# Splitting the output projection of the last attention units, and giving late scores more PSUM tiles

## The chip, the cores and the metric

The kernel runs on one core of a Trainium2 chip. The metric is the device time of one execution in microseconds (us); lower is better. The core's engines work side by side: TensorE (PE, matrix products, with PEld for its weight loads), VectorE (DVE), ScalarE (ACT), GpSimd (POOL) and SyncE (SP, which issues every DMA of this kernel).

## The reference

Two independent results of 2048 x 448 are placed side by side. The first is a state space layer, the second an attention layer with 16 heads of 28:

```python
# a: a kernel K (448 x 2048) made from the parameters, then a long convolution
P = jnp.exp((A * dt[:, None])[:, :, None] * pos[None, None, :])
K = 2.0 * jnp.einsum("dn,dnl->dl", C, P).real
y = jnp.fft.irfft(jnp.fft.rfft(u_t, 4096) * jnp.fft.rfft(K, 4096)[None], 4096)[:, :, :2048]
a = y.transpose(0, 2, 1) + u * D_skip
# b: softmax attention, then the output projection
q, k, v = (x @ wqkv)...                       # 16 heads of 28
p = softmax(q @ k.T * 28 ** -0.5)
b = (p @ v).reshape(B, S, 448) @ wo
out = concatenate([a, b], axis=-1)
```

## The kernel before

The attention is cut into 16 **units**: four groups `g` of four heads times four chunks `c` of 512 queries, `u = 4 g + c`. A unit is walked in 16 **steps** of 128 keys, so that there are 256 steps `s` in one long loop. In a step, for each of the four heads, `s_mm` makes a 128x512 score tile `pss` in PSUM on PE and ACT takes its exponential into `p`. `pv_step` multiplies the `p` of the step before with the values into `po`. Some units ahead of the scores, `max_mm` makes the same scores once more for the row maxima, which DVE (and for some ACT) reduce into `mx`. In the last 18 steps there are no maxima left to make: there the flag `late` is set.

Between these products stand **slots**. The order of one step is written out in `ORDER = ('m0', 's0', 'm1', 's1', 'v', 'f', 'pv', 'f', 'v', 'k', 'm2', 's2', 'm3', 's3', 'v')`: `s` is a score, `m` a maximum, `f` a slot. So one slot stands ahead of `pv_step` and one behind it. In `late` steps a third slot stands at the end of the step. Each slot takes one piece of work, in this order of preference (function `slot`):

1. the `urgent` pieces: the end of a unit's maxima, and `sums` and `scale`, which divide a finished unit's result by its softmax sums and give the tile `on`;
2. `p_due`: the pieces of the output projection that are due at this step;
3. other due lists, empty by the last four units;
4. `f_slot("s")`: the next piece of a **spectrum** job of the convolution;
5. `f_slot("f")`: the next piece of a **finish** job of the convolution.

There are 16 spectrum jobs of four pieces each: two `forth` (products with `yk`, which DVE multiplies into `pr`; behind the second one `join` makes `p` on DVE and POOL), one slot later than the next the two `back` (products of `p`, copied by ACT into `y` and stored to `z`). There are 8 finish jobs of four calls `one(i)` each: a product of `zi` on PE, and an addition of `ut` on DVE into `ot`, which is stored in two halves. Ahead of a job's first call POOL multiplies `ut` with the skip weights. The finish jobs of a half can only start when the eight spectrum jobs of that half are done.

The inputs of a job are loaded by `f_load`, which is called when the job before it has started, and at the earliest three steps (finish) or two steps (spectrum) before the job's own start. The loads of a finish job are `zi` (896 KB) and `ut` (two DMAs, 448 KB together). All DMAs stand in SP's one queue in the order of the program. After the last step the remaining pieces are worked off slot by slot.

Each unit of the last group (`u` = 12 to 15) ends with the output projection of its 512 queries. `load_og(u)` loads the results of the three other groups (`og`, 768 KB); `project(t)` makes, for 128 queries, the products of all four groups with `wo` into one PSUM tile, ACT copies it to `y`, and SP stores it. Each `mm32` product is four matmuls in the program, eight in the trace. So one `project` is 24 matmuls on `og` and 8 on `on` in the trace.

PSUM has eight tiles of 128x512. In this part of the kernel the scores take three in turn (`ps_s`), `po` has one, and four (`w_tile`) serve the maxima and everything in slots. All instructions of this part are kept in the order of the program. They all carry line L75 in the profile, the line of a recording helper, so rows are told apart by tiles.

Of the kernel before, what the change touches and what calls it, by code (L numbers as in the profile page):

```python
# [8 lines left out]
F32 = mybir.dt.float32  # L9
F32R = mybir.dt.float32r  # L10
I32 = mybir.dt.int32
AF = mybir.ActivationFunctionType
ALU = mybir.AluOpType
# [5 lines left out]
D = 448  # L19
# [3 lines left out]
G = 4  # L23
HG = H // G
CQ = 512
NQ = L // CQ
# [10 lines left out]
FX, PD, GAP = 1, 2, 2  # L37
FL = {"s": 2, "f": 3}
S0, SP, SW, SD, PW, E3 = 0, 4, 0, 5, 37, 8
UG = (2, 2, 4)  # L40
PS = 1
SGB, XB, XL = 2, 5, 4
K0, KP, KD, UP = 0, 3.5, 4, 3
A0, A1, KW = 26, 34, (33, 35, 36)
# [46 lines left out]
def body(ctx, tc, a, out):  # L91
    nc = Engines(tc)
    nc.kept = KEPT["p"]
    x, wqkv, wo, u_a = a["B_x"][0], a["B_wqkv"], a["B_wo"], a["A_u"][0]
    out = out[0]

    def pool(stack, name, bufs=1, space=None, side=None):
        kw = {} if space is None else {"space": space}
        if side:
            kw["side"] = side  # L100
        return stack.enter_context(tc.tile_pool(name=name, bufs=bufs, reuse_waits="tile", **kw))
# [23 lines left out]
    def w_tile():  # L125

        n_ring[0] += 1
        return ps_w[0].tile([128, CQ], F32, name=f"pm{n_ring[0] % ps_w[1]}")
# [7 lines left out]
    def mm32(o, w, x_, start, stop, at=0):  # L136

        for i in range(w.shape[-1] // 32):
            c = slice(32 * i, 32 * i + 32)
            nc.tensor.matmul(o[c], w[:, c], x_, start=start, stop=stop, tile_position=(0, at + 32 * i))  # L140
# [13 lines left out]
    def load_v(g, c):  # L154
        v_g[g, c] = t = v_p.tile([128, NK // NQ, HG, 32], F32, name="v", bufs=5)
        nc.sync.dma_start(t.rearrange("p t h e -> p t (h e)"), v_d[c][:, g])
# [55 lines left out]
    with ExitStack() as st:  # L212
# [47 lines left out]
        t = a["A_log_dt"]  # L260
# [261 lines left out]
        def project():  # L522

            e = work.pop(0)() if work else None
            while pend:
                pend.pop(0)()
            if e:
                pend.append(e)
# [29 lines left out]
    ps_s = pool(att, "ps_s", 3, PSUM)  # L558
# [6 lines left out]
    late = [False]  # L565
# [136 lines left out]
    wo_t = []  # L702
# [9 lines left out]
            wo_t.append(t)  # L712

    def s_mm(u, kt, j):
        pss = ps_s.tile([128, CQ], F32, name="pss")
        nc.tensor.matmul(pss, kt_g[u // NQ][j][:, kt * 128:(kt + 1) * 128], q_u[u][:, j, :], start=True, stop=True)
        p = kq_p.tile([128, CQ], F32, name="p", bufs=PB)
        nc.scalar.activation(p, pss, AF.Exp, scale=SCALE)
        return p
# [8 lines left out]
    og_u = {}  # L728

    def load_og(u):  # L730
        og_u[u] = og = kq_p.tile([128, G - 1, CQ], F32, name="og")
        nc.sync.dma_start(og, on_d[u % NQ][:G - 1].rearrange("g p q -> p g q"))

    def fin(u, s_):
        g, c = divmod(u, NQ)
        o = kq_p.tile([128, CQ], F32, name="o")
        nc.scalar.activation(o, o_u[u], AF.Copy)
        on = kq_p.tile([128, CQ], F32, name="on", bufs=2)
        rb = kq_p.tile([128, 4, HG, 32], F32, name="rb")
        og = og_u.pop(u, None)  # L740

        def sums():
            pw = w_tile()
            for t in range(4):
                mm32(pw[:, t * HG:(t + 1) * HG], o[:, t * 128:(t + 1) * 128], sel, start=True, stop=True)
            r = kq_p.tile([128, 4, HG], F32, name="r", bufs=2)
            nc.vector.reciprocal(r, pw[:, :4 * HG].rearrange("p (t h) -> p t h", h=HG))
            nc.scalar.activation(rb, r[:, :, :, None].to_broadcast([128, 4, HG, 32]), AF.Copy)

        def scale():  # L750
            pw = w_tile()
            for t in range(4):
                mm32(pw[:, t * 128:(t + 1) * 128], rb[:, t].rearrange("p h e -> p (h e)"), ident, True, True)
            nc.vector.tensor_tensor(on, o, pw, ALU.mult)
            if g < G - 1:
                nc.sync.dma_start(on_d[c][g], on)
            else:
                p_due.extend((s_ + PD + PS * t, lambda t=t: project(t)) for t in range(4))

        def project(t):  # L760
            pw = w_tile()
            ts = slice(t * 128, (t + 1) * 128)
            for g2 in range(G):
                mm32(pw[:, :D], og[:, g2, ts] if g2 < G - 1 else on[:, ts], wo_t[g2 // 2][:, g2 % 2, :],
                     start=g2 == 0, stop=g2 == G - 1)
            y = kq_p.tile([128, D], F32, name="y", bufs=2)
            nc.scalar.activation(y, pw[:, :D], AF.Copy)
            q0 = c * CQ + t * 128
            nc.sync.dma_start(out[q0:q0 + 128, D:], y)

        soon_slot(UG[1], sums)
        soon_slot(UG[2], scale)

    fk = {}
# [102 lines left out]
    def u_part(i, c):  # L877
        u_jobs[i][1 + c]()
        if c and i not in (14, 15):
            u_load(i + 2)  # L880
        if c and i == 15:
            u_load(16)
            u_load(17)
        if c and i == 31:
            load_wo()
# [15 lines left out]
    f_p, f_ready = {}, {}  # L901

    p_due = collections.deque()
# [37 lines left out]
    def soon_slot(gap, f):  # L941
        n_urgent[0] += 1
        urgent.append((n_slot[0] + gap, n_urgent[0], f))
        q = sorted(urgent)
        urgent.clear()
        urgent.extend(q)

    def slot(s_):
        n_slot[0] += 1
        if urgent and urgent[0][0] <= n_slot[0]:  # L950
            urgent.popleft()[2]()
        elif s_ >= NS and f_slot(s_, "s"):
            pass
        elif p_due and p_due[0][0] <= s_:
            p_due.popleft()[1]()
        elif m_due and m_due[0][0] <= s_:
            m_due.popleft()[1]()
        elif u_due and u_due[0][0] <= s_:
            u_part(*u_due.popleft()[1:])
        else:  # L960
            f_slot(s_, "s") or f_slot(s_, "f")
# [35 lines left out]
    for s in range(NS):  # L997
        u, kt = divmod(s, NK)
        sm = s + NK + min(LEAD, 1 + s // 2)
        more = s in (2, 4)  # L1000
        if s == 12 * NK:
            k0_st.close()
            f_p["s", 0] = f_p["s", 1] = pool(f0_st, "f0_p", side="right")
            f_ready["s", 0], f_ready["s", 1] = s, NS
        if s >= 12 * NK and f_ready["s", 1] == NS and not (k_due or m_due or powers["g"] or powers["e"]):
            g_st.close()
            ps_st.close()
            ps_w[:] = pool(ps_st, "ps_f", 4, PSUM), 1
            f_ready["s", 1] = s + F1
        if kt == 12 and u // NQ == G - 1:  # L1010
            load_og(u)
        late[0] = s + NK + LEAD > NS
        if u % NQ == NQ - 1 and u < NU - 1 and kt % 4 == 2:
            load_v(u // NQ + 1, kt // 4)
        if sm < NS and sm // NK % NQ == NQ - 1 and sm % NK % 4 == 0 and sm % NK and sm // (NQ * NK) + 1 < G:
            load_kd(sm // (NQ * NK) + 1, sm % NK // 4 - 1)
        if sm < NS and sm % (NQ * NK) == 0 and sm:
            load_kd(sm // (NQ * NK), HG - 1)
        if kt % 4 == 1 and u % NQ == 1 and u // NQ + 1 < G:
            load_k(u // NQ + 1, kt // 4, k_pools[(u // NQ + 1) % 2])  # L1020
        if kt == 2:
            if u + 2 < NU:
                load_q(u + 2)
        ps = []
        for op in ORDER:
            if op[0] == "s":
                ps.append(s_mm(u, kt, int(op[1])))
            elif op[0] == "f":
                slot(s)
            elif op[0] == "v":  # L1030
                vec()
            elif op == "k":
                k_next()
                k_begin(s)
                for _ in range(1 if s else 2):
                    k_seed(s)
                for _ in range(3):
                    if powers["e"]:
                        powers["e"].popleft()()
            elif op == "pv":  # L1040
                if prev:
                    pv_step(*prev)
                    if prev[1] == NK - 1:
                        fin(prev[0], s)
            elif sm < NS:
                max_mm(sm // NK, sm % NK - more, int(op[1]))
        for kc in range(4 if more else 0):
            max_mm(1, sm % NK, kc)
        for _ in range(FX if late[0] else 0):
            slot(s)  # L1050
        if sm < NS and sm % NK == NK - 1:
            def end(un=sm // NK):
                max_end(un, w_tile())
                max_put(un)
            max_join(sm // NK)
            soon_slot(UG[0], end)
        k_next()
        prev = (u, kt, ps)
    pv_step(*prev)
    fin(prev[0], NS)  # L1060
    s = NS
# [63 lines left out]
```

## Time and profile before

| | |
|---|---|
| time, median of 3 runs | 1335.06 us (1334.6 to 1336.06) |
| span of the profiled execution | 1335.5 us |
| PE busy | 1238.7 us (93%) |
| DVE, ACT, POOL busy | 990.8, 954.3, 839.3 us |
| mean granted PE clock | 0.972 |
| DMA engines, share of the span | 55.0% for the queue of the kernel's own DMAs |

The profiled execution's span, from its first to its last instruction, lies 0.4 us above the median. In a row of the timeline the first number is the start in us from the span's start, the second the time from the start of the first to the end of the last of the instructions merged into the row, then engine, line, operation, tile written and tiles read, shapes and count; a bracket gives the idle time before it and what ended it. Matmuls overlap, so the distance between two starts tells more of the cost of a piece than the second number. In a row of the windows, each engine's busy time stands in the order PE, PEld, DVE, ACT, POOL, then the granted PE clock, the share of the DMA engines and the GB/s.

### The profile page before, as it was taken

Reading aid. Unit: us, or ns where it says so; the run is one execution under the profiler, and the core shown is the slowest. Engines: PE = TensorE matmul, PEld = TensorE weight load, DVE = VectorE, ACT = ScalarE, POOL = GpSimd, SP = SyncE. Lnnn points to the kernel's source line nnn. Section 1 sums busy time; section 2 is a strip of 40 time slices with the busy share of each in tenths; the row PEclk is TensorE's granted clock in tenths of the full one; section 3 lists DMA queues with packets and bytes.
Section 4 is the critical chain, followed back from the end, with each engine's and each line's share of the span. In section 5 each row is a group of like instructions: output and inputs, shape, how many; then the busy total and the mean of one; then the engine's idle time right before and its main releaser. Section 6 shows DMA issues by size and latency. Waiting matters only on the chain.

```text
span 1335.5 us, 33195 instructions
## 1 busy us (share of the span) xinstructions
PE 1238.7 (93%) x12625; PEld 705.5 (53%) x12625; DVE 990.8 (74%) x2138; ACT 954.3 (71%) x2068; POOL 839.3 (63%) x704
## 2 busy tenths in 40 slices
PE   6879985899999999999989999999998999898998
PEld 5657763455555555555545555555555545444433
DVE  5897887877787777777768889889886858657311
ACT  4875862477788888888878888888885656555553
POOL 3675681388688888788789989999992202202211
PEclk9889987899999999999999999999998999999999
DMA  6677769726765546468634234642424554825485
GB/s 192 208 263 250 240 205 286 202 63 138 177 153 131 113 137 179 129 171 223 165 79 106 61 71 92 143 99 66 100 56 140 191 156 136 256 102 166 149 215 142
DMA packets 200088, 205.36 MB, mean 154 GB/s; under 512 B 95992, under 2 KB 158520, under 8 KB 197880
## 3 DMA queue, kind: packets, MB, share of 16 engines
q1 hardware_dynamic: 199928, 203.23, 55.0%
q8 instruction: 100, 1.64, 0.5%
q14 instruction: 60, 0.49, 0.1%
HBM read 120.73 MB, written 82.18 MB: 152 GB/s over the span
## 4 chain that ended last, share of the span: by engine, by line
PE 67%; DVE 14%; DMA 6%; ACT 5%; POOL 4%; issue 3%; SPq 1%; ACTq 0%; POOLq 0%; DVEq 0%
PE pm L75 37%; PE pss L75 15%; PE po L75 15%; DVE mx L75 2%; DVE tri L75 2%; DMA sdb<-sd 2%; DVE p L75 2%; DVE pr L75 1%; POOL qhat L75 1%; ACT p L75 1%; SPq L75 1%; DVE rl L75 1%; ACT tri L75 1%; DVE qhat L75 1%; DVE sg L75 1%
## 5 line engine op out<-in xcount | busy, mean ns | idle before, releaser
L75 ACT ACTIVATE p<-pss 128x512 f32<-128x512 f32 x1024 | 561.6, 611 | 122.2 <-PE pss L75 117.4
L75 PE MATMUL pss<-qhat,khat 128*128 128x512 f32 x1024 | 405.0, 402 | 10.8 <-ACT p L75 10.6
L75 DVE TENSOR_REDUCE mx<-pm 128x1 f32<-128x512 f32 x500 | 321.5, 684 | 102.8 <-PE pm L75 101.3
L75 PE MATMUL pm<-khat,qhat 128*128 128x512 f32 x749 | 327.5, 439 | 14.7 <-DVE mx L75 7.3
L75 POOL TENSOR_TENSOR e<-e,sdb 128x256 f32<-128x256 f32 x168 | 201.7, 1201 | 134.1 <-ACT e L75 121.3
L75 PE MATMUL po<-p,v 128*32 128x512 f32 x2048 | 271.0, 598 | 0.0
L75 POOL TENSOR_TENSOR e<-e,eu 128x256 f32<-128x256 f32 x168 | 248.3, 1478 | 13.2
L75 PEld LDWEIGHTS pm<-khat,qhat 128*128 128x128 f32 x749 | 141.7, 189 | 212.7 <-ACT p L75 44.4
L75 DVE CUSTOM_DVE_ANT_0 rl<-pm,rl 128x512 f32<-128x512 f32 x249 | 171.5, 689 | 70.7 <-ACT rl L75 64.9
L75 PEld LDWEIGHTS pss<-qhat,khat 128*128 128x128 f32 x1024 | 191.4, 189 | 59.1 <-ACT p L75 19.9
L75 POOL TENSOR_TENSOR eu<-e,sdb 128x256 f32<-128x256 f32 x168 | 202.0, 1202 | 0.0
L75 ACT ACTIVATE rl<-pm 128x512 f32<-128x512 f32 x249 | 151.2, 607 | 20.9 <-PE pm L75 16.5
L75 POOL TENSOR_TENSOR p<-pr,pr 64x448 f32<-64x448 f32 x32 | 40.9, 1278 | 199.0 <-DVE pr L75 187.9
L75 DVE TENSOR_TENSOR g<-g,zg 128x128 f32<-128x128 f32 x392 | 162.1, 414 | 3.5
L75 PE MATMUL pm<-xh,khat 112*128 112x512 f32 x256 | 94.1, 451 | 22.8 <-DVE hl L75 11.0
L75 PE MATMUL pm<-kdif,qhat 128*128 128x512 f32 x249 | 101.0, 405 | 3.4 <-DVE mx L75 1.8
L75 DVE TENSOR_TENSOR zg<-g,zg 128x128 f32<-128x128 f32 x224 | 87.9, 392 | 5.0
L75 PEld LDWEIGHTS pm<-e,g 128*32 128x32 f32 x3584 | 57.5, 110 | 42.1 <-issue 19.4
L75 PEld LDWEIGHTS pm<-xh,khat 112*128 112x128 f32 x256 | 54.1, 217 | 39.1 <-DVE hl L75 12.8
L75 PE MATMUL pm<-e,g 128*32 128x64 f32 x3584 | 73.7, 222 | 0.0
L75 ACT ACTIVATE y<-pm 128x448 f32<-128x448 f32 x48 | 26.3, 548 | 65.9 <-issue 32.7
L75 PEld LDWEIGHTS po<-p,v 128*32 128x32 f32 x2048 | 56.0, 111 | 22.6 <-issue 17.8
(135 smaller groups left out, 1502.4 us busy)
## 6 DMA issues: line engine op xcount, KB each, us to landing
sdb<-sd SPq DMA_DIRECT2D x56, 336.0 KB
khat<-k SPq DMA_DIRECT2D x64, 256.0 KB
qhat<-q SPq DMA_DIRECT2D x64, 256.0 KB
sd<-sg SPq DMA_DIRECT2D x8, 1456.0 KB
k<-hl SPq DMA_DIRECT2D x16, 512.0 KB
q<-hl SPq DMA_DIRECT2D x16, 512.0 KB
mw<-in_mw SPq DMA_DIRECT2D x16, 512.0 KB
sd<-qhat SPq DMA_DIRECT2D x8, 896.0 KB
```

The costliest lines, as they stand in the source:

```text
L75: i = f(*args, **kw)
```

## The change

The output projection of the last four units is made in two parts. `others(u, t)` makes the products of the three other groups and lets DVE copy them to a tile `yp`. It is due in the unit's own steps: the loads of `og` are issued at the unit's first step instead of its thirteenth, and the four calls are due 7, 9, 11 and 13 steps later. `project(t)` then makes only the product of the unit's own group, and DVE adds `yp` to it (before, ACT copied the whole). `p_due` is kept sorted, since it now holds both. In `late` steps, every second score takes a `w_tile` instead of one of the three score tiles.

```diff
+OD = (7, 2)
...
     def s_mm(u, kt, j):
-        pss = ps_s.tile([128, CQ], F32, name="pss")
+        pss = w_tile() if late[0] and j % 2 else ps_s.tile([128, CQ], F32, name="pss")
         nc.tensor.matmul(pss, kt_g[u // NQ][j][:, kt * 128:(kt + 1) * 128], q_u[u][:, j, :], start=True, stop=True)
...
+    def others(u, t):
+        pw = w_tile()
+        for g2 in range(G - 1):
+            mm32(pw[:, :D], og_u[u][:, g2, t * 128:(t + 1) * 128], wo_t[g2 // 2][:, g2 % 2, :], start=g2 == 0, stop=g2 == G - 2)
+        yp_u[u, t] = yp = f_p["s", 0].tile([128, D], F32, name="yp", bufs=4)
+        nc.vector.tensor_copy(yp, pw[:, :D])
+
+    def due_project(s_, f):
+        q = sorted([*p_due, (s_, len(p_seen), f)], key=lambda x: x[:2])
+        p_seen.append(s_)
+        p_due.clear()
+        p_due.extend(q)
...
-                p_due.extend((s_ + PD + PS * t, lambda t=t: project(t)) for t in range(4))
+                for t in range(4):
+                    due_project(s_ + PD + PS * t, lambda t=t: project(t))
...
         def project(t):
             pw = w_tile()
             ts = slice(t * 128, (t + 1) * 128)
-            for g2 in range(G):
-                mm32(pw[:, :D], og[:, g2, ts] if g2 < G - 1 else on[:, ts], wo_t[g2 // 2][:, g2 % 2, :],
-                     start=g2 == 0, stop=g2 == G - 1)
+            mm32(pw[:, :D], on[:, ts], wo_t[g // 2][:, g % 2, :], start=True, stop=True)
             y = kq_p.tile([128, D], F32, name="y", bufs=2)
-            nc.scalar.activation(y, pw[:, :D], AF.Copy)
+            nc.vector.tensor_tensor(y, pw[:, :D], yp_u.pop((u, t)), ALU.add)
...
-        if kt == 12 and u // NQ == G - 1:
+        if kt == 0 and u // NQ == G - 1:
             load_og(u)
+            for t in range(4):
+                due_project(s + OD[0] + OD[1] * t, lambda t=t, u=u: others(u, t))
```

More of the change, by code (lines that the diff above doesn't have):

```diff
@@ L732, in load_og @@
         nc.sync.dma_start(og, on_d[u % NQ][:G - 1].rearrange("g p q -> p g q"))
+    yp_u = {}
+    def others(u, t):
[9 more added lines that the diff above has]
+        p_due.extend(q)
+    p_seen = []
     def fin(u, s_):
@@ L739, in fin @@
         rb = kq_p.tile([128, 4, HG, 32], F32, name="rb")
-        og = og_u.pop(u, None)
         def sums():
@@ L954, in slot @@
         elif p_due and p_due[0][0] <= s_:
-            p_due.popleft()[1]()
+            p_due.popleft()[2]()
         elif m_due and m_due[0][0] <= s_:
```

## The prediction, made before the changed kernel was run

> **What bounds the kernel now.** First the page: busy time by engine, then the chain that ended last.
>
> ```profile
> PE 1238.7 (93%) x12625; PEld 705.5 (53%) x12625; DVE 990.8 (74%) x2138; ACT 954.3 (71%) x2068; POOL 839.3 (63%) x704
> PE 67%; DVE 14%; DMA 6%; ACT 5%; POOL 4%; issue 3%; SPq 1%; ACTq 0%; POOLq 0%; DVEq 0%
> ```
>
> TensorE (PE) carries the kernel. The change touches only the last four units, so I read the timeline there, by steps. A step ends at its `pv_step`, the row `po<-p,v`. A slot after it is called B, a slot before the next one A. The last 18 steps (`late`) have a third slot, X, between the score pairs.
>
> ```profile
> 1028.45 1.04 PE L75 MATMUL po<-p,v 128*32 128x512 f32 x8
> ...
> 1050.35 1.06 PE L75 MATMUL po<-p,v 128*32 128x512 f32 x8
> 1055.93 1.04 PE L75 MATMUL po<-p,v 128*32 128x512 f32 x8
> ...
> 1070.79 1.04 PE L75 MATMUL po<-p,v 128*32 128x512 f32 x8
> 1074.59 0.64 PE L75 MATMUL po<-p,v 128*32 128x512 f32 x4
> ...
> 1084.36 1.04 PE L75 MATMUL po<-p,v 128*32 128x512 f32 x8
> 1093.42 1.04 PE L75 MATMUL po<-p,v 128*32 128x512 f32 x8
> ...
> 1234.21 1.04 PE L75 MATMUL po<-p,v 128*32 128x512 f32 x8
> ...
> 1312.26 1.29 PE L75 MATMUL po<-p,v 128*32 128x512 f32 x7
> ...
> 1317.05 2.44 PE L75 MATMUL pm<-ua,og 128*32 128x448 f32 x24
> 1319.31 0.94 PE L75 MATMUL pm<-ua,on 128*32 128x448 f32 x8
> 1320.06 0.56 PE L75 MATMUL pm<-zi,wb 128*32 128x224 f32 x8
> 1320.43 2.06 PE L75 MATMUL pm<-ua,og 128*32 128x448 f32 x20
> ```
>
> The last four rows price the pieces by the distance of their starts: the other groups' products 2.26 us, the own product 0.75, a `finish` call 0.37. The step 1084.36 to 1093.42 holds two whole projects: 9.06 - 2 x 3.01 = 3.04 us is a bare step (four maxima, four scores, values). The step to 1074.59 holds one `forth`: 3.80 - 3.04 = 0.76. So a step lasts as long as the sum of its PE pieces, unless something stalls it. The step to 1055.93 holds two `back`: 4.56 by the sum, 5.58 in the trace. That 1.0 us is the wait for the joins of the `forth` before, when the slot between them is empty.
>
> **The steps up to the last 18 (1028.45 to 1234.21, 39 steps, 205.8 us).** By these prices 39 bare steps, 8 projects, 54 `forth` and `back`, 4 `finish` calls and some 2 us of small pieces fill 118.6 + 24.1 + 41.0 + 1.5 + 2 = 187 us; 18.6 are stalls. The changed program's instruction order is the same up to the first step of this stretch. In the stretch it has 12 `others` where 8 whole projects stood (+4 x 2.26 = +9.0), and 4 `back`, 3 `forth` and 3 `finish` calls fewer, pushed later (-7 x 0.76 - 3 x 0.37 = -6.4): **+2.6 us** of PE. The stalls shrink. The two worst:
>
> ```profile
> 1156.17 2.34 POOL L75 TENSOR_TENSOR ut<-ut,dsk 128x896 f32<-128x896 f32 x1
> 1158.54 0.39 DVE L75 TENSOR_TENSOR ot<-pm,ut 128x224 f32<-128x224 f32 x1 [1.97 <-POOL ut L75]
> 1158.99 0.58 PE L75 MATMUL pm<-khat,qhat 128*128 128x512 f32 x1 [3.52 <-DVE ot L75]
> ...
> 1213.52 1.04 PE L75 MATMUL po<-p,v 128*32 128x512 f32 x8
> 1219.56 1.03 PE L75 MATMUL po<-p,v 128*32 128x512 f32 x7
> ```
>
> In the first, the first call of a `finish` job stands in slot B right behind a `forth`; VectorE (DVE) waits in order for GpSimd's `ut`, the maxima queue behind it, and PE loses 3.5 us. In the changed order that call stands in slot A, after a step's scores, when `ut` is nearly done: I keep 0.4. The second step holds a `finish` call and a `back`: 4.17 by the sum, 6.04 in the trace; it goes (-1.9), since no other `finish` call is left in this stretch. Of the join waits (about ten, 0.4 to 1.0 us), four get an `others` in their gap, 2.26 us of cover, and two an own product: about -3 us. Together -8, from -11 to -4. Net: **-5.4 us** (bounds -9 to -1).
>
> The evacuations cost little by themselves. DVE gets 16 copies and 16 additions of 128x448, ScalarE (ACT) loses 16 copies. The groups of DVE's instructions from 1000 us on (mean ns behind the comma):
>
> ```profile
> L75 DVE TENSOR_REDUCE mx<-pm 128x1 f32<-128x512 f32 x88 | 56.4, 681 | 31.0 <-PE pm L75 31.0
> ...
> L75 DVE TENSOR_TENSOR p<-pr,pr 64x448 f32<-64x448 f32 x32 | 42.7, 1335 | 0.9
> ...
> L75 DVE TENSOR_TENSOR pr<-pm,ub 128x448 f32<-128x448 f32 x64 | 37.0, 620 | 30.1 <-PE pm L75 30.1
> ```
>
> By the last row that is 32 x 0.62 = 20 us of DVE over some 300. It is hidden as long as PE's step is longer than DVE's; only the steps with a second `forth` beside an own product come close. The `og` load moves twelve steps earlier in SP's queue. Ahead of it is nothing that waits for long, and its tile is free once the last `others` of the unit before has run: nothing.
>
> **The last 18 steps (1234.21 to 1312.26, 78.1 us).** The four `others` of the last unit come in and those of the unit before go out: 0. What was pushed later arrives (+7 x 0.76), and 5 `finish` calls leave (-1.9): +3.4 us of PE. It costs less, since steps without slot work wait anyway:
>
> ```profile
> 1294.73 1.04 PE L75 MATMUL po<-p,v 128*32 128x512 f32 x8
> 1295.70 0.95 PE L75 MATMUL pss<-qhat,khat 128*128 128x512 f32 x3
> 1296.30 2.06 ACT L75 ACTIVATE p<-pss 128x512 f32<-128x512 f32 x4 [1.01 <-PE pss L75]
> 1296.95 0.49 PE L75 MATMUL pss<-qhat,khat 128*128 128x512 f32 x1 [0.29 <-ACT p L75]
> 1297.38 1.11 PE L75 MATMUL po<-p,v 128*32 128x512 f32 x8
> 1298.42 0.96 PE L75 MATMUL pss<-qhat,khat 128*128 128x512 f32 x3
> ```
>
> The fourth score waits for a PSUM buffer (1296.95): the wait that the score edit removes. But `po` at 1297.38 needs the second exponential of the batch, which ends half of 2.06 us after 1296.30, at 1297.33. So the circle score, exponential, values, next score lasts 1.68 + 1.04 = 2.7 us with or without the extra tiles, unless slot work fills it. The tiles give about 0.4 us in each of the four or five steps with one call in slot A: -2. Filled gaps: -1. Sum: **+0.5 us** (bounds -3 to +3; the lower one is no floor, see the first rival).
>
> **Behind the last step (1312.26 to 1335.5, 23.2 us).** PE drops 4 x 2.26 us there. But the slots that `others` took were the slots of `finish`: behind the last unit now stand 13 `finish` calls, before 5. The last two jobs come after everything else, and each job is loaded only when the job before it starts.
>
> ```profile
> 1296.70 0.60 SPq L75 DMA_DIRECT2D og<-on  x1
> ...
> 1306.10 0.56 SPq L75 DMA_DIRECT2D zi<-z  x1
> ...
> 1307.61 2.10 POOL L75 TENSOR_TENSOR ut<-ut,dsk 128x896 f32<-128x896 f32 x1 [10.03 <-DMA ut<-in_A_u]
> ...
> 1314.32 2.08 POOL L75 TENSOR_TENSOR ut<-ut,dsk 128x896 f32<-128x896 f32 x1 [4.61 <-DMA ut<-in_A_u]
> ...
> 1317.37 0.69 DVE L75 TENSOR_TENSOR on<-o,pm 128x512 f32<-128x512 f32 x1 [1.94 <-PE pm L75]
> ...
> 1331.51 1.25 SPq L75 DMA_DIRECT2D out<-ot  x2
> ```
>
> From T0 = 1312.26: `on` is done at T0+5.8 (1317.37 + 0.69); the first own product runs 0.94, its addition 0.62, so the first `out<-y` issues at about T0+7.5. In SP's order the load of the last job but one stands behind that store: T0+7.9. From issue to use such a load took 8.2 us (1306.10 to 1314.32): T0+16.1. The last job's load stands behind three more `y` stores and four `ot` stores, whose issues (1.25 us for two `ot` stores, 1331.51; less for a `y`) and additions put it at T0+13.7. If it takes 8.2 as well, it is there at T0+21.9. But the stores between (3 x 224 + 448 = 1120 KB) and the load (1344 KB) share one queue:
>
> ```profile
> 1304.00:1314.00 10.00, 9.43 (x81) 3.75 (x74) 1.56 (x4) 5.86 (x12) 2.10 (x1) 1.00 0.99 231
> ```
>
> With the DMA engines full (0.99) 231 GB/s moved, so 1120 KB take 5.0 us and the load 6.0: T0+16.1 + 11 = T0+27.1 at worst. I take T0+24.5, between. Then `ut` 2.1, two additions 0.8, four stores of 0.62, and 2.7 us from the last issue to the end as now (1332.76 to 1335.5): T0+32.6 against 23.2, **+9.4 us** (bounds +6.8 to +12.0).
>
> The Trainium skill, page "DMA: Bandwidth & Descriptors", section "Queues, rings and completion order", says that each DMA engine consumes the descriptors of one issuer in ring order; the two loads above, 10.9 us with `og` ahead and 8.2 without, fit it without proving it. Its section "Anatomy of one DMA" gives 2.0 us plus bytes at 436 GB/s (measured there on GpSimd's queue, SP's is used here), by which the load would take an estimated 5.2 us; the 8.2 us here disagree.
>
> **Sum.** -5.4 + 0.5 + 9.4 = +4.5 us. The span of the profiled run is 1335.5, the median of the runs 1335.06: **1339.6 us**, slower by 0.34%. About 0.2% (2.7 us) is what a measurement here can tell from no change.
>
> **Rivals.** *The score tiles free the last steps (faster, 0.20).* If a late step fell to its PE pieces, four scores at (3.04 - 1.04) / 8 = 0.25 and 1.04 for the values (1297.38 to 1298.42), a bare step would be 2.04 instead of 2.65 us. That is 0.6 x 18 = -11 on top: 1329 us; half of it gives 1334. Against it stands the circle above, for it the visible PSUM wait of 0.29. It decides if a step with no slot work takes under 2.3 us. *The last load is not queued (same, 0.17).* At T0+21.9 the tail is +6.8: 1337 us. By the Trainium skill's 5.2 us (same page) it would be at T0+18.9, and the end at 1334. For it: the stores may be spread among the load's packets; against it, the 0.99. *DVE becomes the bound (slower, 0.13).* The join of a second `forth` (2 x 1.34 us), its two products (2 x 0.62), an addition (0.62) and three maxima (3 x 0.68) make 6.6 us in a step of 4.5. If this is not made up in the next step, 2 us in each of three units: 1346. The forecast has 0.50.
>
> **Numbers.** Faster 0.20, same 0.17, slower 0.63. The range 1331 to 1346 leaves out the full first rival and the worst sums.
>
> **What would show it.** Right: the last `po` some 5 us earlier (near 1307); behind it PE nearly idle, 13 `finish` calls, GpSimd waiting for `ut` twice, over 30 us to the end. Steps without slot work still near 2.65. Wrong: a tail below 25 us, because the last two loads came early, or late steps near 2 us; then the kernel is faster. If the last `po` isn't earlier, DVE or the joins ate the filled gaps.

## The result: slower by 0.5%

| | before | changed |
|---|---|---|
| time, median | 1335.56 us (6 runs) | 1341.69 us (6 runs) |
| ratio, 95% interval | 1 | 1.0053 [1.0035, 1.0071] |
| 39 steps up to the last 18 | 205.8 us | 200.2 us |
| last 18 steps | 78.1 us | 79.0 us |
| behind the last `pv_step` (the tail) | 23.2 us | 34.7 us |

The profile after, first the busy time and the chain that ended last:

```profile
PE 1238.8 (93%) x12625; PEld 704.8 (53%) x12625; DVE 1009.8 (75%) x2170; ACT 944.8 (71%) x2052; POOL 839.7 (63%) x704
PE 71%; DVE 13%; ACT 4%; DMA 4%; POOL 4%; issue 3%; SPq 1%; POOLq 0%; DVEq 0%; ACTq 0%
```

PE does the same 12625 matmuls and is busy as long as before (1238.8 us, before 1238.7). DVE is busy 19 us longer, ACT 9.5 us less. Nothing there tells why the kernel is slower; the timeline by stages does. These are the `pv_step` rows that bound the stages (start, length, engine, line, operation):

```profile
1024.24 1.04 PE L76 MATMUL po<-p,v 128*32 128x512 f32 x8
...
1224.43 1.04 PE L76 MATMUL po<-p,v 128*32 128x512 f32 x8
...
1303.45 1.03 PE L76 MATMUL po<-p,v 128*32 128x512 f32 x5
```

The first of them is the row at 1028.45 of before. Up to there PE does the same work in both kernels (only the first `og` load is issued earlier), and the place of the row differs from execution to execution (1024.2 to 1030.5 over the profiles below). So the profiled span, 1338.2 us, shows less of the loss than the medians. From that row to the end it is 307.0 us before and 314.0 after: +6.9 us, which is the 0.5%. (The stretch called the last 18 steps runs between 20 such rows, so it holds 19 steps.)

The loss is in the tail. PE waits there, on loads. The tail's rows in the timeline:

```profile
1310.97 0.36 SPq L76 DMA_DIRECT2D out<-y  x1
1311.42 0.39 SPq L76 DMA_DIRECT2D zi<-z  x1
...
1313.19 0.62 DVE L76 TENSOR_TENSOR y<-pm,yp 128x448 f32<-128x448 f32 x1 [0.81 <-DMA out<-y]
1313.34 0.62 SPq L76 DMA_DIRECT2D out<-y  x1
...
1319.55 2.09 POOL L76 TENSOR_TENSOR ut<-ut,dsk 128x896 f32<-128x896 f32 x1 [10.91 <-DMA ut<-in_A_u]
1319.68 0.62 DVE L76 TENSOR_TENSOR y<-pm,yp 128x448 f32<-128x448 f32 x1 [5.57 <-DMA out<-y]
...
1322.11 0.55 SPq L76 DMA_DIRECT2D zi<-z  x1
...
1328.14 3.21 PE L76 MATMUL pm<-zi,wb 128*32 128x224 f32 x32 [6.06 <-DMA zi<-z]
1330.01 2.08 POOL L76 TENSOR_TENSOR ut<-ut,dsk 128x896 f32<-128x896 f32 x1 [8.38 <-DMA ut<-in_A_u]
1332.13 1.28 DVE L76 TENSOR_TENSOR ot<-pm,ut 128x224 f32<-128x224 f32 x4 [9.18 <-POOL ut L76]
```

The load of the last job but one is issued 8.0 us behind the last `pv_step` (1311.42) and is there at 16.1 (1319.55). The load of the last job is issued at 18.7 (1322.11) and is there at 26.6 (1330.01). Between them stands a wait that I had not seen: there are two `y` tiles, and the fourth addition waits 5.57 us until the second `out<-y` has landed. That store was issued at 1313.34, right behind the big load, and it lands when the load has landed, at 1319.6. SP waits with it, and the last load stands behind it. In the tail by windows (columns as before), PE is busy 2.02 of 5.00 us and 0.08 of 6.00 us while the DMA engines are full (shares 0.99 and 0.97). Between these two stretches, where the last load is not issued yet, the engines are not full (0.38):

```profile
1312.00:1317.00 5.00, 2.02 (x32) 0.74 (x24) 1.29 (x4) 0.00 (x0) 0.00 (x0) 1.00 0.99 269
1319.60:1322.10 2.50, 1.72 (x16) 0.59 (x16) 1.36 (x4) 0.00 (x0) 2.03 (x1) 0.50 0.38 138
1322.00:1328.00 6.00, 0.08 (x4) 0.00 (x0) 0.95 (x4) 0.00 (x0) 0.00 (x0) 0.50 0.97 245
```

### The profile page after: what moved, and what is told of

It reads as the page before. It is cut to its first block, busy times and chain, and to the rows that moved or that the text cites. A ratio compares the mean times of both kernels' runs of the same rounds, so it can differ in the third digit from the quotient of the medians.

```text
span 1338.2 us, 33247 instructions
## 1 busy us (share of the span) xinstructions
PE 1238.8 (93%) x12625; PEld 704.8 (53%) x12625; DVE 1009.8 (75%) x2170; ACT 944.8 (71%) x2052; POOL 839.7 (63%) x704
## 4 chain that ended last, share of the span: by engine, by line
PE 71%; DVE 13%; ACT 4%; DMA 4%; POOL 4%; issue 3%; SPq 1%; POOLq 0%; DVEq 0%; ACTq 0%
PE pm L76 40%; PE po L76 15%; PE pss L76 15%; DVE mx L76 2%; DVE tri L76 2%; POOL qhat L76 1%; DVE p L76 1%; DVE rl L76 1%; ACT p L76 1%; DVE qhat L76 1%; ACT tri L76 1%; DVE pr L76 1%; DVE sg L76 1%; DMA qhat<-q 1%; DMA out<-y 1%
## 5 line engine op out<-in xcount | busy, mean ns | idle before, releaser
L76 ACT ACTIVATE p<-pss 128x512 f32<-128x512 f32 x988 | 544.2, 610 | 138.8 <-PE pss L76 136.0
L76 PE MATMUL pss<-qhat,khat 128*128 128x512 f32 x988 | 395.8, 401 | 6.2 <-ACT p L76 6.1
L76 POOL TENSOR_TENSOR e<-e,eu 128x256 f32<-128x256 f32 x168 | 248.5, 1479 | 13.2
L76 PEld LDWEIGHTS pss<-qhat,khat 128*128 128x128 f32 x988 | 187.0, 189 | 48.4 <-issue 11.3
L76 PE MATMUL pm<-xh,khat 112*128 112x512 f32 x256 | 93.4, 449 | 22.7 <-DVE hl L76 10.9
L76 ACT ACTIVATE ub<-pm 128x224 f32<-128x224 f32 (+1 forms) x96 | 38.7, 448 | 39.8 <-PE pm L76 39.3
```

Source lines behind the costliest of these rows:

```text
L76: i = f(*args, **kw)
```

## The experiments

All stages in us, from the profile of each kernel; the sum runs from the row that starts the 39 steps to the end. The ratio is that of the medians, and a profile is one execution: that of before with the third slot took 1345.4 us where its median is 1351.5, so its stages show only 0.8% of the 1.2%.

| kernel | 39 steps | last 18 | tail | sum | ratio to before |
|---|---|---|---|---|---|
| before | 205.8 | 78.1 | 23.2 | 307.0 | 1 |
| changed | 200.2 | 79.0 | 34.7 | 314.0 | 1.0053 [1.0035, 1.0071] |
| changed, again | 200.2 | 79.3 | 35.3 | 314.8 | 1.0061 [1.0037, 1.0085] |
| split only | 200.2 | 81.9 | 35.6 | 317.6 | 1.0080 [1.0056, 1.0104] |
| score tiles only | 207.1 | 76.8 | 23.2 | 307.1 | 0.9995 [0.9977, 1.0013] |
| sums in place | 199.1 | 78.4 | 33.8 | 311.3 | 1.0037 [1.0021, 1.0053] |
| `others` outside slots | 214.2 | 79.0 | 16.7 | 309.8 | 1.0023 [1.0004, 1.0042] |
| split, third slot | 237.3 | 67.5 | 15.7 | 320.4 | 1.0099 [1.0077, 1.0122] |
| before, third slot | 228.2 | 67.9 | 21.0 | 317.2 | 1.0124 [1.0090, 1.0157] |
| split, loads two ahead | 200.2 | 83.9 | 14.0 | 298.0 | 0.9931 [0.9904, 0.9957] |
| before, loads two ahead | 206.9 | 79.6 | 21.0 | 307.6 | 0.9999 [0.9988, 1.0011] |
| split, two ahead, in place | 199.1 | 83.0 | 12.7 | 294.9 | 0.9890 [0.9874, 0.9906] |

**The two halves of the change, each alone.**

> The changed kernel once more, on the chip of the three experiments beside it. Both theories: 1.003 to 1.007 of the time before, and again some 34 us from the last pv_step to the end.

> The split projection without the score tiles: every score again takes one of the three score tiles. Theory T (the loss lies behind the last step, in the loads of the last finish jobs; the score tiles give little): the last 18 steps grow by 1 to 3 us, the tail stays at 34 to 35 us, the time is 1.006 to 1.008 of before. Rival S (the score tiles free the last steps): the last 18 steps grow by 6 us or more and a step with one finish call goes back to 3.1 us, 1.010 of before or more.

```diff
-        pss = w_tile() if late[0] and j % 2 else ps_s.tile([128, CQ], F32, name="pss")
+        pss = ps_s.tile([128, CQ], F32, name="pss")
```

> The kernel before with the score tiles alone, whole projection as before. Theory T: the last 18 steps are 1 to 3 us shorter, all else the same, 0.998 to 1.000 of before. Rival S: 6 us or more shorter, 0.995 of before or less.

This one is the kernel before with the opposite of that edit. The rows that bound its last 18 steps, and three light steps among them:

```profile
1234.85 1.04 PE L75 MATMUL po<-p,v 128*32 128x512 f32 x8
...
1285.73 1.04 PE L75 MATMUL po<-p,v 128*32 128x512 f32 x8
1287.83 1.66 PE L75 MATMUL po<-p,v 128*32 128x512 f32 x8
1290.94 1.25 PE L75 MATMUL po<-p,v 128*32 128x512 f32 x8
1294.75 1.04 PE L75 MATMUL po<-p,v 128*32 128x512 f32 x8
...
1311.60 0.80 PE L75 MATMUL po<-p,v 128*32 128x512 f32 x3
```

76.8 us against 78.1 without the tiles, and with the split 79.0 to 79.3 against 81.9: the tiles give 1.3 and 2.6 to 2.9 us. The ratio of the tiles alone, 0.9995, can't be told from 1. (Their 39 steps came out 1.3 us longer than before, though the pieces there are the same; the last section has the reason.) The whole loss is the split's. (The tail of the split alone, 35.6 us, is a little above the 34 to 35 expected.) The light steps need care: the step without slot work took 2.65 us before and takes 2.10 here (1285.73 to 1287.83). But its `po` then lasts 1.66 us instead of 1.11, since it starts early and waits inside for the exponentials (the last of them ends at 1289.37). The three steps together last 9.02 us here and 9.35 in the same place of before (to 1294.73, shown in the prediction), whose rows are:

```profile
1285.38 1.04 PE L75 MATMUL po<-p,v 128*32 128x512 f32 x8
1288.02 1.11 PE L75 MATMUL po<-p,v 128*32 128x512 f32 x8
1291.14 1.04 PE L75 MATMUL po<-p,v 128*32 128x512 f32 x8
```

By the prediction's prices their pieces make 7.60 us, so the circle is still there.

**Where the last load waits.** The sum of a projection goes into the `yp` tile, of which there are four.

```diff
-            y = kq_p.tile([128, D], F32, name="y", bufs=2)
-            nc.vector.tensor_tensor(y, pw[:, :D], yp_u.pop((u, t)), ALU.add)
+            y = yp_u.pop((u, t))
+            nc.vector.tensor_tensor(y, pw[:, :D], y, ALU.add)
```

> As the changed kernel, but the sum of a projection is written in place into its yp tile (four buffers) instead of a y tile (two buffers), so that no addition waits for an earlier store of y to land. In the changed kernel the fourth addition waited 5.6 us for such a store, which stood in the DMA queue behind the load of the last job but one, and SP reached the last load 18.7 us after the last pv_step. Here SP reaches it at about 13.7 us. Theory Q (the DMA queue is served in order: the stores between still delay the last load): the load lands at 25 to 27 us as now, the tail stays within 2 us of 34.7, the time falls by 0 to 2 us. Rival P (the place in SP's queue was the delay, the load takes 8 us from its issue): it lands at 21.7 us, the tail is 30 us, the time falls by 5 us.

The last `pv_step`, SP's issue of the last load, GpSimd's start on it, and two windows from the issue of the load before to that start:

```profile
1303.25 1.28 PE L76 MATMUL po<-p,v 128*32 128x512 f32 x7
...
1319.51 0.38 SPq L76 DMA_DIRECT2D zi<-z  x1
...
1328.87 2.09 POOL L76 TENSOR_TENSOR ut<-ut,dsk 128x896 f32<-128x896 f32 x1 [6.91 <-DMA ut<-in_A_u]
...
1312.00:1319.90 7.90, 5.33 (x80) 2.40 (x72) 2.85 (x7) 0.00 (x0) 0.01 (x1) 0.93 0.96 272
1319.90:1328.90 9.00, 1.24 (x16) 0.82 (x20) 1.28 (x4) 0.00 (x0) 2.10 (x2) 0.50 0.94 270
```

SP reaches the load 16.3 us behind the last `pv_step` instead of 18.7, but it is used at 25.6 instead of 26.6: 9.4 us from issue to use, not 8. The tail is 33.8 us. Here the DMA engines are full all the way (0.96 and 0.94, 272 and 270 GB/s), without the gap of the changed kernel. So the stores in between cost their time in the queue, wherever SP stands (theory Q; the landing is in its range, SP's issue came 2.6 us later than expected). Of the tail's 11.5 us, the two `y` tiles made 1 to 1.5. The time fell by 2.4 us against the changed kernel (medians), a little more than the 0 to 2 of theory Q: the 39 steps are 1.1 us shorter too, nearly all of it in one step with two own products (5.77 us from 1164.56 in the changed kernel, 4.70 from 1166.03 here). What shortens that step isn't shown.

**The slots.** `others` is called at the end of its step and takes no slot.

```diff
-            for t in range(4):
-                due_project(s + OD[0] + OD[1] * t, lambda t=t, u=u: others(u, t))
...
+        if u // NQ == G - 1 and kt - OD[0] in (0, 2, 4, 6):
+            others(u, (kt - OD[0]) // 2)
```

> The changed kernel, but the four others calls of a unit take no slot: each is made directly at the end of its step (7, 9, 11 and 13 steps into the unit). The finish calls then stand where they stood before the change, 5 of them behind the last unit. Theory D (the slots that others took pushed the finish jobs behind the last unit): the tail falls from 34.7 to 15 to 18 us; the 39 steps up to the last 18 take 205.8 + 4 x 2.26 less some filled gaps, 209 to 214 us; the time is 0.996 to 1.001 of before. Rival (the tail is long because of the split itself, its additions and its stores): the tail stays above 25 us and the time above 1.005.

The rows of this kernel that bound its stages, and a stall of PE among them:

```profile
1025.37 1.04 PE L76 MATMUL po<-p,v 128*32 128x512 f32 x8
...
1166.40 0.79 PE L76 MATMUL pm<-khat,qhat 128*128 128x512 f32 x1 [3.51 <-DVE ot L76]
...
1239.53 1.04 PE L76 MATMUL po<-p,v 128*32 128x512 f32 x8
...
1318.49 1.03 PE L76 MATMUL po<-p,v 128*32 128x512 f32 x5
```

With the finish calls back in their old places (5 of them behind the last unit, by the matmuls in the trace) the tail is 16.7 us, 18 less than with the change. That shows what made the tail long: not the split's additions or stores, which are still there, but the finish jobs that its slots pushed back. But the 39 steps take 214.2 us, 8.4 more than before, where the three additional `others` that stand in them make 6.8 (the fourth stands just behind their end). So nothing was filled, and the time came out above my range. Counted from the matmuls in the trace, the pieces of the 39 steps weigh 184.4 us before, 187.0 with the change and 191.2 here, by the prediction's prices. The rest of the 39 steps, mostly stalls, is 21.4, 13.2 and 23.0 us. So the 39 steps of the changed kernel were not shorter because work had left them: the pieces that left weigh 6.4 us, the additional `others` 9.0. The stalls had shrunk, and they are back where `others` stands outside the slots; the 3.51 us at 1166.40 are the stall that the prediction read at 1158.99.

**A third slot earlier.** If slots are scarce, give more of them: the third slot of the late steps from the second of the last four units on.

```diff
-        for _ in range(FX if late[0] else 0):
+        for _ in range(FX if late[0] or s >= 13 * NK else 0):
```

> The changed kernel with the third slot of a step from the second unit of the last group on (45 slots more), not only in the last 18 steps. Theory D (slots are what is scarce): no finish call is left behind the last unit, the tail falls to 13 to 17 us, the steps before grow by 3 to 10 us (13 finish calls more, some join waits more), the time is 0.987 to 0.995 of before. Rival (the joins need the distance between slots): the steps before grow by 15 us or more, 0.998 or more.

> The kernel before (whole projection, no score tiles) with the same third slot from the second unit of the last group on. All finish calls are done before the last unit ends; the tail is the four whole projections. Theory D: the tail falls by 2 to 3 us to some 21, the steps before change by -2 to +4, the time is 0.997 to 1.002 of before; so the gain of the third slot is large only together with the split. Rival: the third slot gives its gain by itself, 0.994 or less.

Here my theory fell, and the rival held. The tail is 15.7 us as expected, but the 39 steps take 237.3 and the sum is 6.4 us above that of the changed kernel. By the same count the pieces in the 39 steps grow by 15.5 us (to 202.5), which the later stages save again. The rest grows by 21.6 us (from 13.2 to 34.8), and that is the loss. Rows of the split with the third slot: a step with two `back` and an `others`, a first `finish` call right behind a `forth`, and the last steps.

```profile
1113.62 1.07 PE L76 MATMUL po<-p,v 128*32 128x512 f32 x8
...
1115.41 0.96 PE L76 MATMUL pm<-p,mw 128*32 128x224 f32 x16 [0.72 <-DVE p L76]
...
1121.93 1.04 PE L76 MATMUL po<-p,v 128*32 128x512 f32 x8
...
1170.06 2.34 POOL L76 TENSOR_TENSOR ut<-ut,dsk 128x896 f32<-128x896 f32 x1
1172.42 0.39 DVE L76 TENSOR_TENSOR ot<-pm,ut 128x224 f32<-128x224 f32 x1 [1.97 <-POOL ut L76]
...
1172.87 0.51 PE L76 MATMUL pm<-kdif,qhat 128*128 128x512 f32 x1 [2.79 <-DVE ot L76]
...
1326.05 1.04 PE L76 MATMUL po<-p,v 128*32 128x512 f32 x8
1328.15 1.66 PE L76 MATMUL po<-p,v 128*32 128x512 f32 x8
1330.87 1.65 PE L76 MATMUL po<-p,v 128*32 128x512 f32 x8
```

The step from 1113.62 lasts 8.31 us where its pieces make 3.04 + 2 x 0.76 + 2.26 = 6.82: the `back` follow the `forth` too closely, and the joins on DVE and GpSimd are late (the first `back` waits 0.72 us for one). The second stall is the one that the prediction read at 1158.99, once more. How the 21.6 us divide among such stalls, I haven't worked out. The last steps are not to blame: with nothing in their slots they take 2.1 and 2.7 us (1326.05 to 1330.87), and what the last 18 steps take beyond their pieces is 9.3 us, with the change 10.2. Without the split the same edit costs 1.2%, more than I had allowed for; there too it is the rest of the 39 steps that grows (from 21.4 to 33.3).

**Loads two ahead.** A finish job may be loaded while the job before it still waits for its start; `zi` and `ut` get a third buffer.

```diff
-        if not f_jobs[kind] or f_loaded[kind]:
+        if not f_jobs[kind] or len(f_loaded[kind]) >= (2 if kind == "f" else 1):
...
-            t_["zi"] = p.tile([128, 4, 2, DF], F32, name="zi", bufs=bufs[0])
+            t_["zi"] = p.tile([128, 4, 2, DF], F32, name="zi", bufs=3)
...
-            t_["u"] = p.tile([128, 4, DF], F32, name="ut", bufs=2)
+            t_["u"] = p.tile([128, 4, DF], F32, name="ut", bufs=3)
```

> The changed kernel, but finish jobs are loaded up to two ahead (three zi and ut buffers instead of two), nothing else. The finish calls can then follow each other without the pause of three steps: 2 of them stand behind the last unit. Theory L (the loads that start one job ahead make the tail): the tail falls to 13 to 17 us, the last 18 steps grow by 4 to 12 us (ten more finish calls, and the DMA queue must carry seven jobs in that time), the time is 0.993 to 1.000 of before. Rival (the DMA queue is full anyway, loading earlier only moves the wait into the last steps): the last 18 steps grow by 18 us or more and the time stays above 1.003.

> The kernel before with the finish jobs loaded two ahead, without the split and without the score tiles. It tells whose gain the 0.993 of the split with two loads ahead is. Theory V (the split is worth its gain only where the finish loads don't follow the last unit): without the split the four whole projections stay behind the last unit, the tail is 20 to 21 us, the last 18 steps 78 to 82 us, the time 0.997 to 1.002 of before. Rival (the earlier loads alone are the gain): 0.994 or less.

> The split with the finish jobs loaded two ahead and the sums written in place into the yp tiles. In the split with two loads ahead the third addition of the last unit still waited 1.35 us for a store of y to land. Theory V: that wait goes, the tail falls from 14.0 to 12 to 13 us, 0.991 to 0.993 of before. Rival (the store's landing is the end anyway): no change of the tail.

The split with loads two ahead: the bounds of its last 18 steps, the busy light steps between, and the wait that the in-place version then removes.

```profile
1230.66 1.04 PE L76 MATMUL po<-p,v 128*32 128x512 f32 x8
...
1304.62 1.04 PE L76 MATMUL po<-p,v 128*32 128x512 f32 x8
1308.22 1.04 PE L76 MATMUL po<-p,v 128*32 128x512 f32 x8
...
1314.55 1.03 PE L76 MATMUL po<-p,v 128*32 128x512 f32 x5
...
1324.16 1.39 DVE L76 TENSOR_TENSOR y<-pm,yp 128x448 f32<-128x448 f32 x2 [1.35 <-DMA out<-y]
```

Now each light step at the end holds three `finish` calls in 3.6 us (1304.62 to 1308.22) where several in the changed kernel had one. The last 18 steps have the same number of slots as before this edit, but 29 `finish` calls instead of 18, and 2 instead of 13 are left behind. So in the late steps of the changed kernel slots had stood empty for want of a loaded job. The last 18 steps grow by 4.9 us, and the tail falls from 34.7 to 14.0 us. With the same loads and without the split (and without the score tiles, which alone gave 0.9995) the kernel is where it was: 0.9999. So neither half is worth anything alone here: the change alone costs 0.5%, the loads alone give nothing, and both together give 0.7%. No run separates the third buffers from the earlier loads. With the sums in place it is 1.1%, the best version and better than I had expected: 1322.9 us against 1337.23 us of before on the same chip.

## Why the prediction was right, point by point

- **The 39 steps: -5.4 us forecast, -5.6 measured.** (Two other profiles of the same pieces have 207.1 and 206.9 us, by which it is -6.8.) The two parts came out as well: the pieces grow by 2.6 us as forecast, and the rest shrinks by 8.2 where I had -8. (The trace has 53 `forth` and `back` there, not 54.) The stall of GpSimd's `ut` went, as said, since the first `finish` call now stands in slot A:

```profile
1191.21 1.04 PE L76 MATMUL po<-p,v 128*32 128x512 f32 x8
...
1195.79 1.04 PE L76 MATMUL po<-p,v 128*32 128x512 f32 x8
1196.57 2.36 POOL L76 TENSOR_TENSOR ut<-ut,dsk 128x896 f32<-128x896 f32 x1
1198.96 0.39 DVE L76 TENSOR_TENSOR ot<-pm,ut 128x224 f32<-128x224 f32 x1
```

  That step of the changed kernel lasts 4.58 us (its pieces: 4.17). `ut` is made behind it, later than I had said ("nearly done"), but DVE has other work until 1198.96 and doesn't wait. One part of this stall I had overlooked: towards the end of PE's wait of 3.52 us the granted clock falls to 0.50 (1159.3 to 1162.6). That step of before lasts 8.97 us (1152.45 to 1161.42), 4.80 more than its pieces, so some 1.3 us come on top of the wait. Part of that is the clock: a `back` in it takes 1.72 us (1159.93) instead of 0.96. The windows of before, of the score tiles alone and of the changed kernel:

```profile
1159.30:1162.60 3.30, 3.30 (x26) 1.20 (x28) 1.43 (x4) 1.14 (x2) 0.00 (x0) 0.50 0.33 77
...
1157.70:1164.40 6.70, 6.06 (x43) 2.35 (x43) 2.19 (x5) 1.74 (x3) 0.16 (x1) 0.50 0.50 108
...
1024.30:1224.40 200.10, 192.35 (x1874) 98.33 (x1867) 144.98 (x255) 115.17 (x225) 30.57 (x23) 1.00 0.47 150
```

- **The last 18 steps: +0.5 forecast, +1.0 measured**, and the tiles' 2 us came out as 1.3 and 2.6 to 2.9.
- **The tail: +9.4 forecast, +11.5 measured**, inside the bounds +6.8 to +12.0. This is the term that was undersized. The last load was there at 26.6 us, where I took 24.5 and 27.1 as the worst. The step that failed is SP's place: I let the last load be issued at 13.7 us, and it was issued at 18.7. Without the wait for a `y` tile (in place) it is 16.3. There SP issues one DMA behind the other for 7.5 us between the issues of the two loads (1311.99 to 1319.51), where I had allowed 5.8; the first of them is 0.8 us later than I said. The issue-to-use time was 8 us, as before the change, and not the 10.8 that I had reckoned from issue to landing, because the queue had run empty during that wait (the window with 0.38). That the two errors nearly cancel is luck; the in-place run shows the case that I had reckoned (a load behind the stores, 25.6 us). One reading of the prediction was off as well: its 10.9 us with `og` ahead count from the issue of `og`; from the load's own issue (1297.40) to its use (1307.61) it is 10.2.
- **The first rival** (score tiles free the last steps) fell: 1.3 us alone, 0.9995. But its deciding test was badly chosen. In the run with the tiles alone a step without slot work does take 2.10 us, under my 2.3, because the start of `po` moves and not its end. A test by one start mark would have misled; the sum over three steps decides.
- **The second** (the last load is not queued) fell by the in-place run. The Trainium skill, page "DMA: Bandwidth & Descriptors", section "Queues, rings and completion order", says that each DMA engine consumes the descriptors of one issuer in ring order; the store issued at 1313.34 that lands with the load ahead of it, at 1319.6, agrees.
- **The third** (DVE becomes the bound) didn't show. With 19 us more work on DVE the 39 steps are shorter, and between 1025 and 1234 us PE waits 5.0 us for DVE instead of 10.8. The steps of this stretch with an own product and a `forth` last at most 0.4 us longer than their pieces.

## What to carry to other kernels

Where small pieces share slots that are handed out by priority, a piece that is moved forward moves another one back. Follow the order to its end and see what comes last there; if that has a load in front of it that starts one job ahead, its latency stands bare behind the last matmul. Cut the waits of the pushed-back work first (here: load two jobs ahead, a buffer for each store in flight), and the same change that cost 0.5% gives 1.1%.

## What the runs showed of the hardware

- A 224 KB store queued right behind a 1344 KB load took 6.3 us from its issue to the release of its buffer (1313.34 to 1319.68). In a tail, the reuse of a store's buffer is priced by what stands ahead of the store.
- In the tail the granted PE clock fell to 0.50 while PE was nearly idle (1322 to 1328), and the last 32 matmuls of `finish` ran at a slow pace behind it (3.21 us at 1328.14, by the price of 0.37 a call 1.48). It cost nothing here, since GpSimd's `ut` was later still.
- A wait of PE can cost more than its length. In the four profiles where PE waits 3.5 us for `ot` (before, score tiles only, before with loads two ahead, `others` outside the slots), the granted clock falls to 0.50 about the end of the wait and stays there for 3.4 or 6.8 us. In the changed kernel, without that wait, it is 1.00 through the whole 39 steps. The longer fall is why the 39 steps took 207.1 us in the run with the score tiles alone and 205.8 before: the two steps at the stall last 14.9 us there (1151.80 to 1166.72) and 13.6 before (1152.45 to 1166.09). How long a wait brings the fall isn't settled here: in the split with the third slot PE waited 2.79 us at 1172.87, and the clock did not fall.
